# One of a quad's 32 exponential tiles moved from ScalarE to GpSimd as a power of two, with a reordered quad and GpSimd in written order

## The chip, the core and the metric

The kernel runs on one core of a Trainium2 chip. The metric is the device time of one execution in microseconds (us), here the median of the runs shown. TensorE (PE) multiplies matrices into PSUM, ScalarE (ACT) applies functions such as the exponential, VectorE (DVE) and GpSimd (POOL) do elementwise work, SyncE (SP) issues the transfers, which 16 DMA engines carry. PEld is the loading of weights into PE.

## What is computed

Four residual layers over a sequence of 2048 rows of 512 numbers, with 32 heads of 16. Layers 0 and 2 attend within a window of 256 keys, layers 1 and 3 over all 2048 keys.

```python
def _B_ref(x, wqkv, wo):                      # _A_ref: the same with a causal window of 256
    qkv = (x @ wqkv).reshape(B, S, 3, H, Dh) ...
    scores = jnp.einsum("bhqd,bhkd->bhqk", q, k) * Dh ** -0.5
    p = softmax(scores)
    o = jnp.einsum("bhqk,bhkd->bhqd", p, v)
    return o.transpose(...).reshape(B, S, D) @ wo
x = x + _A_ref(_layernorm(x), A_wqkv, A_wo)
x = x + _B_ref(_layernorm(x), B_wqkv, B_wo)
x = x + _A_ref(_layernorm(x), A_wqkv, A_wo)
x = x + _B_ref(_layernorm(x), B_wqkv, B_wo)
```

## The kernel before

**A quad.** The full layers (1 and 3) work by chunks `c` of 512 queries and, in a chunk, by quads `qd` of four heads: 4 x 8 quads in a layer. A quad goes through 16 key tiles `j` of 128 keys. For each `j` there are two pairs of heads `pr`, and for each pair one score tile `s` of 128 x 1024 (128 keys, two heads by 512 queries), so a quad has 32 score tiles. `exps` (L714) makes a score tile: PE writes it by eight matmuls into one of two PSUM buffers (`ps_s`), and ACT reads it and writes the exponential `e` to SBUF (L735), into one of six buffers (`EB`). A score tile can be written when ACT has read the one two before it. The queries and keys have been extended beforehand by rows that hold a bound, so that the scores come out already shifted and no row maximum is taken.

**The product with the values.** `attn_full` (L767) runs the 16 steps. Its product with the values of step `j` (the `pv` of a step, L779: eight matmuls in the program, 16 in the records, into the two accumulators `acc`) comes later than its exponentials. `attention` keeps products in a line `pvq`, and `flush(1)` lets all but the youngest go whenever a step has written its first score tile (the `yield None` after pair 0). So in the steady state PE's order is: score tile (j,0), product j-2, score tile (j,1), side work, score tile (j+1,0). After the last product of a quad, `epilogue` (L683) has DVE add the two accumulators (`sa`, L415 and L416), transpose, and divide by the sum; the next quad's first product overwrites the accumulators and so waits for `sa`.

**Side work.** Beside the quads, `Side` hands PE small pieces of the projections of this and of the next layers (`project`, `values`, `wo`, `wo_part`), eight or sixteen matmuls at a time between two score tiles. In the full layers they all go through one PSUM tile of two banks, `PH["halves"]` (the side bank, named `b` in the trace). When one of its results is complete, DVE reads both banks (`join`, or L677 and L653), and only then can PE write the next one. What is left of a chunk's side work at the chunk's end (in layer 1: at the layer's end) is done there by `sd.finish()`, one piece after the other, with no score tile between.

**Order.** In the full layers PE and DVE run in the order in which the program issues them. The planner keeps a clock (`clock[0]`, 1.8 us a step) and its estimates of when DVE is free (`vt_`) and results are ready, and places the pieces by them. The orders of ACT, POOL and SP are made by a scheduler, and each engine and queue takes its instructions strictly in its order.

**Loads.** `load_full` (L744) loads a quad's queries `qt` (256 KB, two buffers) and its keys as two halves `kt` of 512 KB (key tiles 0 to 7 and 8 to 15) in a ring of three buffers. The second half for a quad goes into the buffer that the first half of the quad before it held, so it can be loaded only when that quad has written its last score tile from key tiles 0 to 7. All these loads are issued by SP.

**POOL** in the full layers has only the squares of queries and keys (`sq`, L521), whose sums PE takes by `hsum` (L543), and the low halves of the outputs (`oh`, L712).

Of the kernel before, what the change touches and what calls it, by code (L numbers as in the profile page):

```python
# [9 lines left out]
F32 = mybir.dt.float32  # L10
# [23 lines left out]
EB, XB, XNB, WB, VB, OB = 6, 4, 4, 2, 3, 5  # L34
RINGS = WB, VB
L_MIN = 2.0 ** -90
# [153 lines left out]
def fast_path(ctx, tc, flag, a_x, a_wqkv, a_wo, b_wqkv, b_wo, out):  # L190
# [13 lines left out]
    ctx.push(ps_x)  # L204
    dp = pool("scr", 1, space=bass.MemoryType.DRAM)
# [5 lines left out]
    XC, XN, V, O, OT, KM, PH = {}, {}, {}, {}, {}, {}, {"free": 0.0, "busy": False}  # L211
    WT, ST, pend = {}, {}, []
    VQ, vt_ = [deque() for _ in range(4)], [0.0]
# [15 lines left out]
    def soon(chain, us, f):  # L229

        if PH["full"]:
            VQ[chain].append((clock[0], us, f))
        else:
            f()

    def drain(upto=None):

        if upto is not None:
            for q in VQ[:upto]:
                while q:  # L240
                    vec(q[0][1])
                    q.popleft()[2]()
            return
        while vt_[0] <= clock[0] + 0.2:
            q = next((q for q in VQ if q), None)
            if q is None:
                return
            vec(q[0][1])
            q.popleft()[2]()
# [21 lines left out]
    zeros = cp.tile([P, QC], F16, name="zeros")  # L271
# [15 lines left out]
    nc.gpsimd.memset(zeros, 0.0)  # L287
# [15 lines left out]
    def fill(t, key, c0=0, c1=1):  # L303
        r4 = lambda d0, d1: rows(t).rearrange("h (d b) (c n) -> h d b c n", b=4, n=QC)[:, d0:d1, 3]
        for c in range(c0, c1):
            if key:
                nc.sync.dma_start(r4(0, 1)[:, 0, c], ones[:H])
                nc.sync.dma_start(r4(1, DH)[:, :, c], zeros[:H, None, :].broadcast_to([H, DH - 1, QC]))
            else:
                nc.sync.dma_start(r4(1, DH)[:, :, c], ones[:H, None, :].broadcast_to([H, DH - 1, QC]))  # L310
# [31 lines left out]
    def verify(ty, s):  # L342

        am = vp.tile([P, D], F32, name=f"wa{ty}_{s}", tag="wa", bufs=1)
        for k in range(NC):
# [4 lines left out]
            yield from turns(3, (1.1, lambda: nc.vector.tensor_reduce(am[:, f], raw.rearrange("p k f -> p f k"), axis=AX.X, op=ALU.max,  # L350
                                                                      apply_absolute_value=True)))

        def bounds():
            at = vp.tile([P, D], F32, name=f"wt{ty}_{s}", tag="wc", bufs=1)
            nc.vector.transpose(at, am)
            mx = vp.tile([P, D // 32], F32, name=f"wx{ty}_{s}", tag="wx")
            nc.vector.tensor_reduce(mx, at.rearrange("p (b r) -> p b r", r=32), axis=AX.X, op=ALU.max)
            nc.vector.tensor_tensor(wlow, wlow, mx, ALU.min)
            nc.vector.tensor_tensor(whigh, whigh, mx, ALU.max)
        yield from turns(3, (1.8, bounds))  # L360
# [12 lines left out]
    def phase(l):  # L373

        PH["full"], PH["win"] = l is not None and l % 2 == 1, l is not None and l % 2 == 0
# [53 lines left out]
    def norm(l, c, xs, tail=False):  # L429

        mv, y, nb, out = ST[l, c][1], [], [], []

        def scales():
            y.append(rsqrt(nc, vp, f"{l}_{c}", mv[:, :, 1]))
# [4 lines left out]
        def parts(i):  # L439
            xn = vp.tile([P, D], F32, name=f"xn{l}_{c}_{i}", tag="xn", bufs=1)  # L440
# [37 lines left out]
    def project(l, s, c, act, ht=None):  # L478
# [5 lines left out]
        xc = XC[l, c]  # L484
        if s == 0:
# [6 lines left out]
        for t in range(NHT) if ht is None else (ht,):  # L492
# [19 lines left out]
            def parts(t=t, sp=None if full else sp, j=j if full else None):  # L512
                if full:
                    sp = vp.tile([P, 2, QC], F16, name=f"sp{n}_{t}", tag="sp", bufs=3)
                    nc.vector.tensor_copy(sp[:, 0], j)  # L515
                    nc.vector.tensor_tensor(sp[:, 1], j, sp[:, 0], ALU.subtract)
                sq = vp.tile([P, QC], BF16, name=f"sq{n}_{t}", tag="sq", bufs=NHT)
# [77 lines left out]
    def key_shift(l, ht=None):  # L595
# [6 lines left out]
        nc.vector.tensor_scalar(m[r], ones[r], kx[r], -0.515, op0=ALU.mult, op1=ALU.mult)  # L602
# [39 lines left out]
    def wo(l, c, tail):  # L642
# [4 lines left out]
        for i in range(4):  # L647
# [11 lines left out]
            yield -MM if PH["full"] else -12 * MM  # L659
        if PH["full"]:  # L660
            yield from norm(l + 1, c, xs, tail)

    def wo_part(c, t):
# [6 lines left out]
        for i in range(4):  # L670
# [7 lines left out]
            nc.sync.dma_start(out[0, k * P:(k + 1) * P, :] if t == NHT - 1 else xd[k], xs[i])  # L678
            yield -MM

    def epilogue(l, c, qd, a):
# [25 lines left out]
        def parts():  # L707
            o = vp.tile([P, QC], F32, name=f"o{n}", tag="o", bufs=1)
            nc.vector.transpose(o, OT.pop(t).rearrange("p b u d -> p (b u d)"))
            hl = O[l, c, t] = wp.tile([P, 2, QC], F16, name=f"oh{n}", tag="ohl", bufs=OB)  # L710
# [4 lines left out]
        if u:  # L715
            soon(1, 1.2, parts)

    def exps(name, kt, qt, pr, pieces):
# [15 lines left out]
        e = pp.tile([P, 2, QC], F32, name=f"e{name}", tag="e", bufs=EB)  # L734
        nc.scalar.activation(e[:, :, w0:w1], ps[:, :, w0:w1], AF.Exp, scale=SCALE)  # L735
        return e

# [29 lines left out]
    def attn_full(l, c, qd, kt, qt, a):  # L767
        for j in range(NT):
            es_ = []
            for pr in range(2):  # L770
# [4 lines left out]
            def pv(j=j, es_=es_):  # L775
                for h in range(4):
                    for r in range(2):
                        k = slice(R * r, R * r + R)
                        nc.tensor.matmul(acc[r][32 * h:32 * h + DH + 1, :], V[l, qd // 4, j // 8][k, j % 8, 4 * (qd % 4) + h, :],  # L779
                                         es_[h // 2][k, h % 2, :], start=(j == 0), stop=(j == NT - 1),  # L780
# [39 lines left out]
    class Work:  # L820
# [7 lines left out]
        def ready_at(self):  # L828
# [12 lines left out]

            if self.norm and not self.begun and NB:
# [40 lines left out]
    class Side:  # L883
# [65 lines left out]
        def share(self):  # L949

            self.budget = min(self.budget + max((self.cost - self.spent) / max(self.steps - 3 - self.k, 1), self.least), 0.75)
            self.lag = max(self.lag - 0.42, -0.3)
            if pend and not PH["busy"] and clock[0] >= max(PH["free"], pend[0][0]):
# [32 lines left out]
    def attention(l, works):  # L986
# [5 lines left out]
        for t in range(NHT if l == 3 else 1):  # L992
            for c in range(NQ):
                qds = range(2 * t, 2 * t + 2) if l == 3 else range(NQD)
                if l == 1:

                    sd = sd or Side(NT * NQD // 2, works[0], works[1], 0.33)
                    while ("Q", 1, c) not in DONE:
# [4 lines left out]
                ops = load(l, c, qds[0])  # L1003
                for qd in qds:
# [4 lines left out]
                    a = acc[qd % 2 if win else 0]  # L1009
                    began, u = clock[0], 0  # L1010
                    for f in (attn_win if win else attn_full)(l, c, qd, *ops, a):
# [6 lines left out]
                        clock[0] = max(clock[0], began + (2.4 if win else 1.8))  # L1018
# [16 lines left out]
                if not win:  # L1035
# [155 lines left out]
    for l in range(4):  # L1191
# [5 lines left out]
        else:  # L1197
            with tc.manual_schedule(engines={mybir.EngineType.PE, mybir.EngineType.DVE}):
# [42 lines left out]
```

## Time and profile before

| what | value |
|---|---|
| runs | 2759.74 and 2760.26 us, median 2760.0 us |
| the profiled execution | 2759.5 us, span 2757.7 us |
| granted TensorE clock, mean | 0.988 |
| busy share of the span | PE 91%, ACT 86%, DVE 40%, PEld 40%, POOL 19% |

The page gives the busy time of each engine, the span in 40 slices of 69 us with a digit for the busy tenths of each engine, the chain of work that ended last, and the groups of instructions with their mean durations and the idle time ahead of them. In the timeline a row is: start, duration, engine, line, operation, output and inputs, how many, and in brackets the idle time ahead and what ended it. Matmuls overlap in the array, so PE's speed is read from the distance between starts, not from the duration of one. ACT's records overlap as well: the distance of two starts is what a tile costs.

### The profile page before, as it was taken

To read this page: it belongs to the slowest core of one execution; us is meant where nothing else is said; L and a number is where in the kernel's file an instruction comes from. 1 tells how busy PE (TensorE), PEld (TensorE's weight loads), DVE (VectorE), ACT (ScalarE), POOL (GpSimd) and SP (SyncE) were. 2 spreads that over 40 slices of the span, in tenths; PEclk is the share of its full clock that TensorE was granted. 3 is DMA by queue.
4 is the path that set the end of the run, shared out by engine and by line. 5 is a ranking of instruction groups with operands and counts; after the bars stand their busy time and mean duration, and the time that the engine had idled before them with its cause. 6 is when DMAs were issued, how large, how long until landed. Compare 5 with 4: busy or idle time off the path is not lost.

```text
span 2757.7 us, 112292 instructions
## 1 busy us (share of the span) xinstructions
PE 2496.1 (91%) x50513; PEld 1100.3 (40%) x50513; DVE 1094.9 (40%) x2314; ACT 2362.9 (86%) x2683; POOL 515.8 (19%) x1074
## 2 busy tenths in 40 slices
PE   7888989999989999999998898899899999998987
PEld 3233334444433344444443333534444444433332
DVE  5564554122343335325326566323333333333333
ACT  4556654899999999999995667399999999999997
POOL 1445552001000000100105678100000000000000
PEclk9999999999999999999999999999999999999999
DMA  8888856322342224324225565623232333333332
GB/s 286 226 241 240 244 178 191 96 83 82 100 120 79 86 93 137 102 78 126 93 73 169 157 181 143 175 72 109 84 107 90 98 97 104 112 104 123 114 120 103
DMA packets 335035, 359.67 MB, mean 130 GB/s; under 512 B 113616, under 2 KB 250320, under 8 KB 328144
## 3 DMA queue, kind: packets, MB, share of 16 engines
q1 hardware_dynamic: 334544, 352.40, 42.3%
q8 instruction: 397, 6.50, 1.0%
q14 instruction: 94, 0.77, 0.1%
HBM read 239.60 MB, written 96.99 MB: 122 GB/s over the span
## 4 chain that ended last, share of the span: by engine, by line
ACT 56%; PE 23%; issue 11%; DVE 5%; DMA 3%; POOL 2%; SPq 0%; ACTq 0%; DVEq 0%; POOLq 0%
ACT e L735 55%; PE b L402 10%; PE acc L812 3%; PE acc L779 3%; PE bs L402 2%; PE s L731 2%; PE s L727 2%; PE b L399 1%; POOL e L802 1%; POOL e L805 1%; DMA qt<-qs 1%; DMA kt<-kw 0%; DMA wr<-in_A_wo_dram 0%; DVE ot L694 0%; DMA w<-wd 0%
## 5 line engine op out<-in xcount | busy, mean ns | idle before, releaser
L735 ACT ACTIVATE e<-s 128x1024 f32<-128x1024 f32 (+2 forms) x2432 | 2238.8, 1058 | 121.0 <-PE s L731 95.3
L779 PE MATMUL acc<-e,vt 64*17 64x512 f32 x16384 | 1085.0, 590 | 1.3 <-issue 1.3
L727 PE MATMUL s<-qt,kt 64*32 64x512 f16 x16384 | 849.0, 380 | 130.4 <-ACT e L735 106.6
L727 PEld LDWEIGHTS <-kt 64*32 64x32 f16 x16384 | 406.7, 89 | 944.2 <-issue 868.8
L779 PEld LDWEIGHTS acc<-e,vt 64*17 64x17 f32 x16384 | 280.5, 92 | 61.1 <-issue 1.5
L805 POOL TENSOR_SCALAR_AFFINE_SELECT e<-e 128x256 f32<-128x256 f32 x512 | 224.9, 446 | 196.5 <-ACT e L735 195.4
L802 POOL TENSOR_SCALAR_AFFINE_SELECT e<-e 128x256 f32<-128x256 f32 x448 | 198.1, 449 | 114.1 <-ACT e L735 112.3
L712 POOL TENSOR_TENSOR oh<-o,oh 128x512 f16<-128x512 f32 x31 | 36.1, 1165 | 938.1 <-DVE oh L711 884.8
L812 PE MATMUL acc<-e,vt 128*17 128x384 f32 (+2 forms) x2816 | 204.7, 396 | 5.3 <-POOL e L802 4.0
L731 PE MATMUL s<-qt,kt 64*128 64x384 f16 (+2 forms) x1408 | 129.0, 280 | 64.0 <-ACT e L735 38.2
L415 DVE TENSOR_SCALAR sa<-acc 128x512 f32<-128x512 f32 x64 | 44.3, 692 | 335.4 <-PE acc L779 335.4
L402 PE MATMUL b<-xc,w 128*128 128x512 f16 x696 | 166.1, 390 | 7.0 <-DMA w<-wd 5.8
L677 DVE SCALAR_TENSOR_TENSOR x<-b,x 128x512 f32<-128x512 f32 x122 | 83.9, 688 | 193.0 <-PE b L399 189.8
L402 PEld LDWEIGHTS <-w 128*128 128x128 f16 x816 | 77.4, 100 | 122.8 <-issue 35.8
L521 POOL TENSOR_TENSOR sq<-sp 128x512 bf16<-128x512 f16 x28 | 41.0, 1463 | 442.2 <-DVE sp L515 427.6
L506 ACT ACTIVATE sp<-b 128x512 f16<-128x512 f32 x58 | 34.7, 598 | 103.3 <-PE b L402 91.2
L731 PEld LDWEIGHTS <-kt 64*128 64x128 f16 x1408 | 54.4, 94 | 167.6 <-issue 137.0
L521 POOL TENSOR_TENSOR sq_h<-sp_h 128x512 bf16<-128x512 f16 x27 | 40.1, 1484 | 409.8 <-DVE sp_h L515 409.8
L399 PE MATMUL b<-wo,oh 64*32 64x512 f16 x2592 | 109.9, 376 | 6.2 <-DVE x L677 3.1
L399 PE MATMUL b<-xc,w 64*32 64x512 f16 x2688 | 110.9, 376 | 3.0 <-DVE j L416 2.3
L399 PE MATMUL b<-xc,w_h 64*32 64x512 f16 x2592 | 104.4, 376 | 4.1 <-DVE km L562 3.9
L415 DVE TENSOR_SCALAR j_h<-b 128x512 f32<-128x512 f32 x27 | 18.7, 691 | 218.7 <-PE b L399 187.6
(136 smaller groups left out, 1874.8 us busy)
## 6 DMA issues: line engine op xcount, KB each, us to landing
kt<-kf SPq DMA_DIRECT2D x128, 512.0 KB
qt<-qs SPq DMA_DIRECT2D x128, 256.0 KB
xd<-x SPq DMA_DIRECT2D x96, 256.0 KB
x<-xd SPq DMA_DIRECT2D x96, 256.0 KB
w<-wd SPq DMA_DIRECT2D x22, 1024.0 KB
kt<-kw SPq DMA_DIRECT2D x64, 256.0 KB
qs<-sp SPq DMA_DIRECT2D x48, 256.0 KB
wo<-wd SPq DMA_DIRECT2D x12, 1024.0 KB
```

Of the source, the lines that this page charges most:

```text
L399: nc.tensor.matmul(ps[g:g + 32, r], a[k, g:g + 32], b[k], start=(i == 0), stop=(i == len(pairs) - 1), skip_group_check=True)
L402: nc.tensor.matmul(ps, a, b, start=(i == 0), stop=(i == len(pairs) - 1))
L415: nc.vector.tensor_scalar(dst, ps[0], scale, None, op0=ALU.mult)
L521: nc.gpsimd.tensor_tensor(sq, sp[:, 0], sp[:, 0], ALU.mult)
L677: nc.vector.scalar_tensor_tensor(xs[i], p, 1 / WS, xs[i], op0=ALU.mult, op1=ALU.add)
L727: nc.tensor.matmul(ps[g:g + 32, h], kt[R * h:R * h + R, pr, kc + g:kc + g + 32], qt[R * h:R * h + R, pr], start=True, stop=True, skip_grou ...
L731: nc.tensor.matmul(ps[:, h, s0:s0 + wd_], kt[R * h:R * h + R, pr, kc:kc + P], qt[R * h:R * h + R, pr, qc:qc + wd_], start=True, stop=True)
L735: nc.scalar.activation(e[:, :, w0:w1], ps[:, :, w0:w1], AF.Exp, scale=SCALE)
L779: nc.tensor.matmul(acc[r][32 * h:32 * h + DH + 1, :], V[l, qd // 4, j // 8][k, j % 8, 4 * (qd % 4) + h, :], es_[h // 2][k, h % 2, :], star ...
L802: nc.gpsimd.affine_select(v, v, pattern=[[0, 2], [-1, P]], compare_op=ALU.is_gt, fill=0.0, base=0, channel_multiplier=1)
L805: nc.gpsimd.affine_select(v, v, pattern=[[0, 2], [1, P]], compare_op=ALU.is_ge, fill=0.0, base=0, channel_multiplier=-1)
L812: nc.tensor.matmul(a[32 * h:32 * h + DH + 1, q * P:(q + nb) * P], V[l, (4 * c + j) // 4][:, j % 4, 4 * qd + h, :], es_[h // 2][:, h % 2, s ...
```

## The change

In the full layers, key tile `DJ` = 7 is taken out of its place and done last in the quad (`js`). Of its two score tiles, the one of pair 0 no longer goes to ACT. `unit` has PE write it, at some earlier step, into the side bank; DVE scales it by SCALE times log2(e), clamps it at -126 and writes it to SBUF (a new tile `d`, two buffers); POOL raises two to it, in place, in two instructions of 128 x 512. The product of key tile 7 then reads `d` for pair 0 and ACT's `e` for pair 1. `units` decides at which step: for the next quad from 6 us (by the planner's clock) into the present one, as soon as the side bank is free, and for the first quad of a chunk at once. The planner's own cost for POOL's two instructions is `XP` = 9.0. The last step of a quad has one ACT tile, no `yield None`, and is planned as 0.9 us.

POOL joins PE and DVE in running in written order. The `e` tiles get a pool of their own, with six buffers in the window layers and five in the full ones. To make room, `zeros` becomes a part of `ones` and the weight check (`verify`) works in tiles of 128 columns: 32 times five DVE instructions instead of 32 plus 8 times four. `key_shift` takes one small DVE instruction more. The planner gets a few conditions: an output tile is not overwritten before it has been used (`OFREE`), sums of squares wait for POOL's planned time (`PH["sq"]`), and side work is held while a unit waits for the side bank. All 64 quads of the two layers have a unit in the changed program: ACT has 64 instructions fewer, DVE 64 and POOL 128 more for it.

```diff
-EB, XB, XNB, WB, VB, OB = 6, 4, 4, 2, 3, 5
+EB, XB, XNB, WB, VB, OB = (6, 5), 4, 4, 2, 3, 5
+DJ = NT // 2 - 1
+UNITS = 1
+XP = 9.0
...
+    def unit(u):
+        pr = len(u["e"])
+        ps = PH["halves"]
+        for g in range(0, P, 32):
+            for h in range(2):
+                nc.tensor.matmul(ps[g:g + 32, h], u["kt"][R * h:R * h + R, pr, DJ % 8 * P + g:DJ % 8 * P + g + 32],
+                                 u["qt"][R * h:R * h + R, pr], start=True, stop=True, skip_group_check=True)
+        spent(0.27)
+        vec(1.4)
+        PH["free"] = max(clock[0] + 0.6, vt_[0])
+        t = PH["ep"].tile([P, 2, QC], F32, name=f"d{n}", tag="d", bufs=2)
+        nc.vector.tensor_scalar(t, ps, SCALE * LOG2E, -126.0, op0=ALU.mult, op1=ALU.max)
+        pt_[0] = max(pt_[0], vt_[0]) + XP
+        for h in range(2):
+            nc.gpsimd.tensor_tensor(t[:, h], two.broadcast_to([P, QC]), t[:, h], ALU.pow)
+        u["e"].append(t)
...
     def attn_full(l, c, qd, kt, qt, a):
-        for j in range(NT):
+        js = [j for j in range(NT) if j != DJ] + [DJ]
+        for j in js:
             es_ = []
-            for pr in range(2):
+            if j == DJ:
+                es_ = list(UX.popleft()["e"])
+            PH["step"] = 1.8 - 0.9 * len(es_)
+            for pr in range(len(es_), 2):
                 es_.append(exps(f"{l}_{c}_{qd}_{j}_{pr}", kt[j // 8], qt, pr, [(j % 8 * P, 0, QC, 0)]))
                 if pr == 0:
                     yield None
...
-                                         es_[h // 2][k, h % 2, :], start=(j == 0), stop=(j == NT - 1),
+                                         es_[h // 2][k, h % 2, :], start=(j == js[0]), stop=(j == js[-1]),
...
+                if not win:
+                    expect(l, c, qds[0], *ops, 0.0)
...
+                    if nxt and not win:
+                        expect(l, c, qd + 1, *nxt, 6.0)
...
-            with tc.manual_schedule(engines={mybir.EngineType.PE, mybir.EngineType.DVE}):
+            with tc.manual_schedule(engines={mybir.EngineType.PE, mybir.EngineType.DVE, mybir.EngineType.Pool}):
```

**Where it moves instructions: the end of a quad.** This is PE's order from quad 2 to quad 3 of chunk 1 in layer 1, one row for each run of like rows. A name `s_1_2_15_1` is chunk, quad, key tile and pair (the last number is the buffer's); a row that reads `s` stands for the eight matmuls of a score tile, a row on `acc` for the four matmuls with one of a step's two exponential tiles. Before:

```order
L727 MATMUL s_1_2_15_1_13728<-qt_1_2_12382,kt_1_2_1_12386 32x512
...
L727 MATMUL s_1_3_0_0_13745<-qt_1_3_13088,kt_1_3_0_13090 32x512
...
L779 MATMUL acc_81<-e_1_2_14_0_13678,vt_0_1_5232 17x512
...
L779 MATMUL acc_81<-e_1_2_14_1_13702,vt_0_1_5232 17x512
...
L727 MATMUL s_1_3_0_1_13769<-qt_1_3_13088,kt_1_3_0_13090 32x512
...
L779 MATMUL acc_81<-e_1_2_15_0_13713,vt_0_1_5232 17x512
...
L779 MATMUL acc_81<-e_1_2_15_1_13737,vt_0_1_5232 17x512
...
L727 MATMUL s_1_3_1_0_13793<-qt_1_3_13088,kt_1_3_0_13090 32x512
```

And at the same place in the changed program:

```order
L755 MATMUL s_1_2_7_1_13668<-qt_1_2_12304,kt_1_2_0_12306 32x512
...
L755 MATMUL s_1_3_0_0_13701<-qt_1_3_13012,kt_1_3_0_13014 32x512
...
L847 MATMUL acc_81<-e_1_2_14_0_13599,vt_0_1_5230 17x512
...
L847 MATMUL acc_81<-e_1_2_14_1_13618,vt_0_1_5230 17x512
...
L847 MATMUL acc_81<-e_1_2_15_0_13631,vt_0_1_5230 17x512
...
L847 MATMUL acc_81<-e_1_2_15_1_13650,vt_0_1_5230 17x512
...
L755 MATMUL s_1_3_0_1_13728<-qt_1_3_13012,kt_1_3_0_13014 32x512
...
L847 MATMUL acc_81<-d_1_2_0_12758,vt_0_0_4501 17x512
...
L847 MATMUL acc_81<-e_1_2_7_1_13677,vt_0_0_4501 17x512
...
L755 MATMUL s_1_3_1_0_13752<-qt_1_3_13012,kt_1_3_0_13014 32x512
```

The quad now ends with a single score tile, after which no product is let go. The two products that wait then (14 and 15) both stand between the next quad's first and second score tile, where one stood before. The same holds at all 62 places where a quad follows a quad in its layer. The last score tile of the quad also reads `kt_1_2_0`, the first half of the keys, which before had its last reader at key tile 7 in the middle of the quad.

**The end of layer 1**, on PE. Before, the last score tile is followed by the last two products:

```order
L727 MATMUL s_3_7_15_1_28645<-qt_3_7_27293,kt_3_7_1_27297 32x512
...
L779 MATMUL acc_81<-e_3_7_14_0_28605,vt_1_1_5653 17x512
...
L779 MATMUL acc_81<-e_3_7_14_1_28624,vt_1_1_5653 17x512
...
L779 MATMUL acc_81<-e_3_7_15_0_28635,vt_1_1_5653 17x512
...
L779 MATMUL acc_81<-e_3_7_15_1_28654,vt_1_1_5653 17x512
```

In the changed program 304 matmuls of side work (the values of layer 2's chunk 2, in the side bank, 96 for each filling) and the sums of squares `sq` stand there first:

```order
L755 MATMUL s_3_7_7_1_28525<-qt_3_7_27124,kt_3_7_0_27126 32x512
...
L417 MATMUL b_5730<-wv_2_0_0_26774,xc_2_25732 32x512
...
L566 MATMUL b_5730<-sq_1_2_0_27285,hsum 32x512
...
L847 MATMUL acc_81<-e_3_7_14_0_28442,vt_1_1_5658 17x512
...
L847 MATMUL acc_81<-e_3_7_14_1_28461,vt_1_1_5658 17x512
```

Such a run of side work without score tiles also stands at the ends of two chunks of layer 3, where there was none before: 160 matmuls of 256 columns (values) after quad 3 of chunk 1, and 96 of 512 columns (`wo`, 24 for each filling) with 192 of 256 columns (values) after quad 3 of chunk 3.

**SP's order** in layer 3, chunk 0, around the loads for its quad 5. Before, the second half of quad 4's keys, three rows on other data, then quad 5's queries and the first half of its keys:

```order
L752 DMA kt_0_4_1_44441<-kf 128x2x1024
L588 DMA qs_0_101<-m_0_2_44109 8x512
...
L748 DMA qt_0_5_44443<-qs_0_101 128x2x512
L752 DMA kt_0_5_0_44445<-kf 128x2x1024
...
L752 DMA kt_0_5_1_44447<-kf 128x2x1024
```

In the changed program:

```order
L816 DMA kt_0_4_1_44707<-kf 128x2x1024
L812 DMA qt_0_5_44709<-qs_0_101 128x2x512
L816 DMA kt_0_5_0_44711<-kf 128x2x1024
L703 DMA xd<-x_12_44320 128x512
L482 DMA x_0_44795<-xd 128x512
...
L816 DMA kt_0_5_1_44713<-kf 128x2x1024
```

The first of these rows now waits for the last score tile of the quad before, and the two behind it wait with it; `unit` of quad 5 reads their data six score tiles later. In layer 3 seven such units stand six tiles after the release, in layer 1 five stand eight tiles after it, the others ten or more.

105 lines of the change are left out of this document (74 added, 31 removed).

## The prediction

> **What bounds the kernel now.** I read the page first (busy shares and slices), then ACT's exponentials by stage, then the chain of waits and the timeline of one quad's end.
>
> ```profile
> span 2757.7 us, 112292 instructions
> PE 2496.1 (91%) x50513; PEld 1100.3 (40%) x50513; DVE 1094.9 (40%) x2314; ACT 2362.9 (86%) x2683; POOL 515.8 (19%) x1074
> ACT  4556654899999999999995667399999999999997
> POOL 1445552001000000100105678100000000000000
> L735 ACT ACTIVATE e<-s 128x1024 f32<-128x1024 f32 (+2 forms) x2432 | 2238.8, 1058 | 121.0 <-PE s L731 95.3
> ```
>
> The two stretches of 9s in ACT's row are the full layers, which hold two thirds of the span. There POOL is nearly idle. The stages of ACT's line, columns: span, ACT busy and count, granted clock, DMA share, GB/s:
>
> ```profile
> 1100.00:1300.00 200.00, 198.22 (x216) 1.00 0.34 102
> 2100.00:2300.00 200.00, 197.28 (x215) 1.00 0.31 93
> ```
>
> In both layers ACT is busy 99% of the time with exponentials alone: it is the bound, and 216 tiles in 200 us leave next to nothing between them. The busy share of PE over the whole span says less, since its matmuls overlap. What one tile costs, and how close PE follows, is read in the chain of waits (start, duration, what) and the timeline, at a place where one quad follows another in layer 1:
>
> ```profile
> 701.16 0.87 ACT e L735
> ...
> 702.08 0.71 ACT e L735
> ...
> 703.00 0.87 ACT e L735
> ...
> 703.91 1.03 ACT e L735
> 704.94 0.04 issue
> 704.98 0.60 ACT e L735
> ```
>
> ```profile
> 702.30 0.41 PE L727 MATMUL s<-qt,kt 64*32 64x512 f16 x8 [0.35 <-ACT e L735]
> 702.51 1.05 PE L779 MATMUL acc<-e,vt 64*17 64x512 f32 x16
> 703.37 0.41 PE L727 MATMUL s<-qt,kt 64*32 64x512 f16 x8
> 703.59 1.05 PE L779 MATMUL acc<-e,vt 64*17 64x512 f32 x16
> 704.44 0.41 PE L727 MATMUL s<-qt,kt 64*32 64x512 f16 x8
> 704.66 0.63 PE L399 MATMUL b<-xc,w 64*32 64x512 f16 x16
> 704.74 0.69 DVE L415 TENSOR_SCALAR sa<-acc 128x512 f32<-128x512 f32 x1 [1.88 <-PE acc L779]
> 705.09 0.41 PE L727 MATMUL s<-qt,kt 64*32 64x512 f16 x8
> ```
>
> Five prices follow, from starts. A tile costs ACT (703.91 - 702.08) / 2 = 0.915 us. A score tile costs PE 0.21 (702.30 to 702.51), a product with the values 0.86 (702.51 to 703.37), sixteen side matmuls 0.43 (704.66 to 705.09). ACT starts at the earliest 0.54 after PE starts the tile (704.44 to 704.98), and PE may refill a buffer 1.14 after ACT started on it (701.16 to 702.30). So a buffer's circle takes 1.14 + 0.54 = 1.68 of the 1.83 that two tiles give: PE may be 0.15 late, no more. The third tile here was late: 704.98 where 703.91 + 0.915 = 704.82 was due. A quad's end costs 0.16 before the change.
>
> **The sum.** It is made against the profiled execution, 2759.5 us (span 2757.7), which lies 0.5 under the median of 2760.0.
>
> *ACT loses 64 tiles:* 64 x 0.915 = **-58.6 us**. That is the ceiling, 2.1%.
>
> *The quad's end.* I count from ACT's start on the last tile before key tile 7's (0.00), with the prices above. The single tile of key tile 7 follows at 0.92. PE can write the next quad's first tile at 1.14; ACT takes it at 1.83, in time. Behind it now stand two products: 1.14 + 0.21 + 2 x 0.86 = 3.07 for the second tile, so ACT starts it at 3.61, where 2.75 was due. The product of key tile 7 follows (3.07 + 0.21 + 0.86 = 4.14), the third tile reaches ACT at 4.68 instead of 3.61 + 0.915 = 4.53. Together 1.02 late, against 0.16 before: 0.86 at each of 62 places, **+53.3**. The reason is the missing pause after a single tile; a slack of 0.15 cannot hide a product of 0.86. So the end of the quad gives back nearly the whole tile.
>
> *The unit's own work.* PE writes the same eight matmuls as before, in a slot that side work would have had: 0 while that slot exists. In the first quad of 15 chunks of layer 3 it stands between the next quad's second tile and the last product, where there is no slot: 0.21, and DVE reads the side bank ahead of `sa`, so the accumulators come free about 0.25 later. 15 x 0.46 = **+7**. DVE's reading of 1024 numbers from PSUM costs what `km` of the same size does:
>
> ```profile
> L562 DVE TENSOR_REDUCE km<-b 128x1 f32<-128x1024 f32 x3 | 3.7, 1225 | 5.0 <-PE b L543 5.0
> L712 POOL TENSOR_TENSOR oh<-o,oh 128x512 f16<-128x512 f32 x31 | 36.1, 1165 | 938.1 <-DVE oh L711 884.8
> L521 POOL TENSOR_TENSOR sq<-sp 128x512 bf16<-128x512 f16 x28 | 41.0, 1463 | 442.2 <-DVE sp L515 427.6
> L677 DVE SCALAR_TENSOR_TENSOR x<-b,x 128x512 f32<-128x512 f32 x122 | 83.9, 688 | 193.0 <-PE b L399 189.8
> ```
>
> 64 x 1.23 on an engine that is 40% busy is hidden, apart from the places named. No row shows a power. POOL's nearest instructions of the size take 1.17 and 1.46, so a unit takes at least 2.3 us; the planner charges 9.0. I take 9.0, since a power is more work than a product. It is hidden either way: a quad lasts 32 x 0.915 = 29 us, and its product of key tile 7 stands at least 17 score tiles (15 us) after that in nearly all quads, so up to some 24 us it would cost nothing. `sq` and `oh` queue behind it on POOL; their readers on PE stand 3 or more score tiles after they would be done at 9.0, save three `sq` behind which PE waits today as well, 1.2 us in all:
>
> ```profile
> L543 PE MATMUL b<-sq_h,hsum 64*32 64x512 bf16 x54 | 10.3, 377 | 2.1 <-POOL sq_h L521 1.2 <-DVE x L677 0.8 <-DVE vt L416 0.2
> ```
>
> That makes 0 for POOL.
>
> *Left-over side work.* The orders show three runs without score tiles that were not there. Each filling of the side bank ends in two DVE instructions (0.69 each by L677's row) and some 0.25 of signals, 1.65 in all, before PE may write again. End of layer 1: 304 matmuls, 304 / 16 x 0.43 = 8.2, four turns 6.6, one product more 0.9: 15.7. Layer 3, 160 matmuls of half the columns: 2.2 and one turn of half size 1.1, less the 0.7 that PE waits there anyway: 2.6. Layer 3, 96 and 192: 2.6 + four turns 6.6 + 2.6 + 1.1 - 0.7 = 12.2. Sum **+30.5**, since ACT has nothing to do meanwhile. At the very end of layer 3 one more turn, a product and eight matmuls: **+3**.
>
> *The loads.* At a quad's end SP now issues three loads at once, 512, 256 and 512 KB, 1.31 MB. What the queue moves in such a burst (core's row: span, then busy times, clock, DMA share, GB/s):
>
> ```profile
> 705.00:709.00 4.00, 3.88 (x120) 1.82 (x111) 2.88 (x8) 4.00 (x5) 0.00 (x0) 1.00 0.81 252
> 760.80:767.20 6.40, 4.70 (x112) 1.91 (x111) 4.39 (x10) 6.40 (x8) 0.00 (x0) 1.00 0.51 166
> ```
>
> The second row holds an issue of 1 MB from its first to its last byte, 166 GB/s x 6.4 us. At that rate 1.31 MB takes 7.9 us; at the 252 GB/s of the first row, inside a burst, 5.2. From the release at 0.7 on the count above the data is there at 5.9 to 8.6. A unit six tiles on is due at 7.5 (six tiles of 0.915 and the lost 1.02 after 1.14), one eight tiles on at 9.4. So seven units wait 0 to 1.1, and PE and with it ACT wait too; should a second transfer of 256 KB lie between, 1.6 more. I take 1.1 for six of the seven (one stands behind left-over work), **+7**; between 0 and 17. The five buffers of `e` delay the next quad's first tile by 0.2, within the 0.86 already lost. The weight check's additional instructions lie on DVE beside a layer of 950 us: 0.
>
> Sum: -58.6 + 53.3 + 7 + 30.5 + 3 + 7 = +42, **2802 us**, 1.5% slower.
>
> **The port rule.** POOL is busy in the window layer in the middle of the span (5 to 8 tenths in its row of slices), with short instructions, and the same DVE instruction, two inputs from SBUF, takes longer there. DVE's row in 1100 to 1300 us, then in 1500 to 1700, then POOL's instruction:
>
> ```profile
> L699 DVE TENSOR_TENSOR lsum<-lsum,ot 128x16 f32<-128x16 f32 x6 | 1.1, 179 | 0.0
> ```
>
> ```profile
> L699 DVE TENSOR_TENSOR lsum<-lsum,ot 128x16 f32<-128x16 f32 x22 | 7.2, 326 | 0.0
> ```
>
> ```profile
> L805 POOL TENSOR_SCALAR_AFFINE_SELECT e<-e 128x256 f32<-128x256 f32 x512 | 224.9, 446 | 196.5 <-ACT e L735 195.4
> ```
>
> It is 0.15 us longer beside POOL instructions of 0.45: what a wait for the rest of one would give. The Trainium skill has the rule for it (SBUF — State Buffer, Who interferes with whom): the port pair that the two engines share is held for a whole instruction, and a VectorE instruction with two SBUF inputs waits until a GpSimd instruction that reads SBUF is done. The trace agrees in direction; how long a power would hold it no run here shows.
>
> **Rivals.**
> 1. *POOL holds DVE up.* In the first quad of a chunk in layer 3, `lmin`, `lsum` and `op` stand on DVE between the two units' readings. If they wait for both halves of the first power (till 14 us on the count above at 9.0), the second unit's reading ends at about 16, and PE, which needs the side bank at some 13, waits 3: seven to 15 places, +20 to +45, 2822 to 2847; I write 2830. For it: the row of `lsum`. Against it: the power may be shorter, and POOL may let DVE in between.
> 2. *Not slower: the second product is hidden.* If PE got both products done before the tile was due, the 53.3 would go and the sum would be 2749; at 0.18 per place instead of 0.86 it breaks even. It needs score buffers that are free earlier; the row at 702.30, where PE waits 0.35 for ACT, speaks against it.
> 3. *The loads and left-overs cost less:* the loads land at 252 GB/s, and half of the left-over work overlaps: -22, 2780.
> 4. *The power takes over 24 us:* key tile 7's product waits in the first quads and the squares with it; at 30 us some 6 us in 16 quads, 2900.
>
> **How the numbers follow.** Chances: the forecast 0.47, rival 1 0.27, rival 2 0.08, rival 3 0.14, rival 4 0.04. The forecast's own range is 2788 to 2820 (0.1 on 0.86 at 62 places, and the loads from 0 to 17). The range of 2770 to 2842 takes in rival 3 and most of rival 1. Two per cent, about what a measurement of this kernel can tell from no change, ends at 2704.8 and 2815.2. Faster by that much would need the whole ceiling: 0.02. Slower: 0.18 of the forecast's 0.47, 0.23 of rival 1, rival 4: 0.45. Within: 0.53.
>
> **What would show it.** Right: at a quad's end ACT's starts show 1.8 us once where 0.92 is usual; the chain has PE's share up and ACT's down; 64 exponentials fewer; a gap in ACT of some 15 us at the end of layer 1. Wrong: starts at a quad's end that keep 0.92; PE rows of unit or product that wait for POOL; `lmin` rows on DVE of several us, which is rival 1.

## The result, and the profile after

The changed kernel takes 11950.2 us (11947.05 and 11953.27), 4.33 times the time before, with an interval of 4.311 to 4.348. The forecast was 2802.

The page of the changed kernel: busy time of the engines, three rows of slices (one slice is now 299 us), the chain that ended last, and six groups of instructions (busy, mean ns of one, then the idle time ahead of them and what ended it).

```profile
PE 2704.2 (23%) x50513; PEld 1134.0 (9%) x50513; DVE 1189.3 (10%) x2479; ACT 2329.1 (19%) x2619; POOL 10980.0 (92%) x1203
ACT  5411111211111112112341111211012111021110
POOL 4599999999999999999878999898998889988889
PEclk9865555655666556656785555656556555565555
POOL 79%; issue 10%; PE 6%; ACT 3%; DVE 1%; DMA 1%; SPq 0%; ACTq 0%; DVEq 0%; POOLq 0%
L782 POOL TENSOR_TENSOR d<-two,d 128x512 f32<-128x512 f32 x128 | 10482.9, 81917 | 439.4 <-DVE d L779 439.4
L763 ACT ACTIVATE e<-s 128x1024 f32<-128x1024 f32 (+2 forms) x2368 | 2205.7, 1049 | 9205.3 <-PE s L755 8762.3
L847 PE MATMUL acc<-d,vt 64*17 64x512 f32 x512 | 174.5, 866 | 5128.9 <-POOL d L782 5128.9
L566 PE MATMUL b<-sq_h,hsum 64*32 64x512 bf16 x54 | 13.7, 498 | 2842.5 <-POOL sq_h L544 2840.8
L566 PE MATMUL b<-sq,hsum 64*32 64x512 bf16 x56 | 11.6, 505 | 864.5 <-POOL sq L544 861.5
L417 PE MATMUL b<-wo,oh 64*32 64x512 f16 x2592 | 126.0, 394 | 154.3 <-POOL oh L740 145.9
```

The bound has changed its engine. POOL's row reads 8 and 9 through both full layers, where it read 0 and 1, and ACT's reads mostly 1 and 2, where it read 9. The row of L782 says why: one power of 128 x 512 takes 81.9 us, a unit 163.8, where 9.0 had been taken. The 128 powers are 10483 of the 11945 us. The last four rows show how POOL's time reaches the others. PE waits 5129 us for the product of key tile 7. It waits 2841 and 862 us for squares (`sq_h` and `sq`), instructions of 1.1 to 1.2 us that stand behind powers in POOL's order, and 146 us for the low halves of the outputs. Together that is 8977 us. ACT's 9205 us of idle time are nearly all (8762) ended by PE's next score tile: PE stands, so nothing comes.

Two answers of the trace on the rival in which POOL holds DVE up. First POOL's row in the timeline (start, duration), then DVE's rows inside it:

```profile
663.02 163.81 POOL L782 TENSOR_TENSOR d<-two,d 128x512 f32<-128x512 f32 x2
```

```profile
667.85 0.18 DVE L725 TENSOR_TENSOR lmin<-lmin,ot 128x16 f32<-128x16 f32 x1
667.95 0.17 DVE L726 TENSOR_TENSOR lsum<-lsum,ot 128x16 f32<-128x16 f32 x1
668.53 0.43 DVE L732 TENSOR_TENSOR op<-ot,r 128x256 f32<-128x256 f32 x1
```

DVE instructions with two inputs from SBUF run at their usual length 5 us into a power that lasts another 77. Of each of these three lines, 46 instructions in the whole trace lie inside a power; the longest took 0.19, 0.19 and 0.43 us. DVE was not held.

### The profile page after: what moved, and what is told of

It is laid out like the page before. It is cut to its first block, busy times and chain, and to the rows that moved or that the text cites. A ratio compares the mean times of both kernels' runs of the same rounds, so it can differ in the third digit from the quotient of the medians.

```text
span 11945.3 us, 112446 instructions
## 1 busy us (share of the span) xinstructions
PE 2704.2 (23%) x50513; PEld 1134.0 (9%) x50513; DVE 1189.3 (10%) x2479; ACT 2329.1 (19%) x2619; POOL 10980.0 (92%) x1203
## 4 chain that ended last, share of the span: by engine, by line
POOL 79%; issue 10%; PE 6%; ACT 3%; DVE 1%; DMA 1%; SPq 0%; ACTq 0%; DVEq 0%; POOLq 0%
POOL d L782 79%; ACT e L763 3%; PE b L420 2%; PE acc L847 1%; PE acc L880 1%; PE s L755 0%; PE bs L420 0%; PE s L759 0%; POOL oh L740 0%; PE b L417 0%; DVE d L779 0%; POOL sq L544 0%; POOL sq_h L544 0%; POOL e L873 0%; POOL e L870 0%
## 5 line engine op out<-in xcount | busy, mean ns | idle before, releaser
L782 POOL TENSOR_TENSOR d<-two,d 128x512 f32<-128x512 f32 x128 | 10482.9, 81917 | 439.4 <-DVE d L779 439.4
L763 ACT ACTIVATE e<-s 128x1024 f32<-128x1024 f32 (+2 forms) x2368 | 2205.7, 1049 | 9205.3 <-PE s L755 8762.3
L847 PE MATMUL acc<-d,vt 64*17 64x512 f32 x512 | 174.5, 866 | 5128.9 <-POOL d L782 5128.9
L847 PE MATMUL acc<-e,vt 64*17 64x512 f32 x15872 | 1169.7, 619 | 0.7 <-issue 0.7
L755 PE MATMUL s<-qt,kt 64*32 64x512 f16 x15872 | 924.2, 400 | 123.5 <-ACT e L763 104.4
L566 PE MATMUL b<-sq_h,hsum 64*32 64x512 bf16 x54 | 13.7, 498 | 2842.5 <-POOL sq_h L544 2840.8
L585 DVE TENSOR_REDUCE km<-b 32x1 f32<-32x1024 f32 (+3 forms) x26 | 25.8, 991 | 1352.7 <-PE b L566 1206.9
```

What stands on the lines that cost most here:

```text
L755: nc.tensor.matmul(ps[g:g + 32, h], kt[R * h:R * h + R, pr, kc + g:kc + g + 32], qt[R * h:R * h + R, pr], start=True, stop=True, skip_grou ...
L782: nc.gpsimd.tensor_tensor(t[:, h], two.broadcast_to([P, QC]), t[:, h], ALU.pow)
```

## The experiments

**1. Only the power's duration taken away.** A multiplication of the same inputs in its place; all orders stay.

```diff
-        nc.vector.tensor_scalar(t, ps, SCALE * LOG2E, -126.0, op0=ALU.mult, op1=ALU.max)
+        nc.vector.tensor_scalar(t, ps, SCALE * LOG2E, 0.5, op0=ALU.mult, op1=ALU.max)
...
-            nc.gpsimd.tensor_tensor(t[:, h], two.broadcast_to([P, QC]), t[:, h], ALU.pow)
+            nc.gpsimd.tensor_tensor(t[:, h], two.broadcast_to([P, QC]), t[:, h], ALU.mult)
```

> The changed kernel with POOL's power replaced by a multiplication of the same two inputs and size, and DVE's clamp at 0.5 in place of -126 so that the numbers stay positive; it leaves the power out, all else and every order stays. Theory A, the power's own duration (81.92 us for one of 128 x 512, 164 for a unit) is all that went wrong, and the other terms of the sum hold: 2802 us, ACT's starts at a quad's end show 1.8 us once, some 15.7 us without tiles at the end of layer 1. Rival B, the second product at a quad's end is hidden: 2749. Rival C, something besides the power's duration holds the changed kernel up (the written order of POOL, the waits of the squares): several thousand us still, or well above 2850.

Measured: 2806.6 us, 1.0156 of the time before (1.0139 to 1.0173). Theory A holds to 5 us: 9144 us of the changed kernel's time are the power's duration, and what is left is the forecast's own sum (its terms follow further down). POOL's and ACT's rows with the multiplication, and the chain of waits over one quad's end:

```profile
L782 POOL TENSOR_TENSOR d<-two,d 128x512 f32<-128x512 f32 x128 | 132.3, 1054 | 760.0 <-DVE d L779 727.7 <-DVE v L49 31.1 <-DVE kx L604 1.2
L763 ACT ACTIVATE e<-s 128x1024 f32<-128x1024 f32 (+2 forms) x2368 | 2196.9, 1052 | 201.7 <-PE s L759 116.5 <-PE acc L847 52.0 <-PE s L755 20.2
```

```profile
1030.80 1.10 ACT e L763
...
1031.94 0.41 PE s L755 x8
1032.35 0.89 PE acc L847 x12
...
1033.32 1.02 ACT e L763
...
1034.41 1.03 ACT e L763
...
1035.48 0.60 ACT e L763
```

The forecast counted from ACT's start on the tile ahead of key tile 7's, here 1030.80 (the single tile of key tile 7 runs beside PE's rows and is not on the chain). The next quad's second tile was to start 3.61 later, the third 4.68. They start at 1034.41 and 1035.48: 3.61 and 4.68. The first tile was put at 1.83 and starts at 2.52: its buffer is the fifth one back, which the product of key tile 14 still reads, and ACT's row names that product for 52 us of its idle time. Since the second tile is late by PE's order anyway, this costs nothing further.

**2. One product behind the single tile.** A pause after it as well, so that the bunched products are spread.

```diff
-            for pr in range(len(es_), 2):
+            for pr in range(first, 2):
...
-                if pr == 0:
+                if pr == first:
                     yield None
```

> As the one with the multiplication (the power is left out), and the quad's last step pauses after its single tile as well, so that by PE's order one product, not two, stands between the first and the second score tile of the next quad at 62 places. Theory A, a second product of 0.86 us costs its full length at each place: 53 us less than without the pause, about 2749. Rival B, the second product was hidden, or its wait comes back at the next tile: no more than 10 us less.

Measured: 2818.3 us, 1.0203 (1.0186 to 1.0220), so 12 us slower than without the pause. Theory A falls, and B does not say why it is slower. The profiled execution is the fastest of the four, 2812.1 us, and so only 6 us slower than the one profiled without the pause. By ACT's starts it spends 6.5 us less in layer 1 (939.1 for 945.6), 3.7 less in layer 3 (975.7 for 979.4) and 6.6 less ahead of and between them, but 22.9 more after layer 3's last score tile (48.6 for 25.7). Two things work against each other. The loss at a quad's end shrinks only in part, from 1.02 us to a median of 0.75 in layer 1: three products (14, 15 and 7) still stand between four tiles, since the program lets the last one go at the end of the next quad's first step. And the planner, asked to go on at other points, leaves 224 matmuls of side work for the very end instead of 56. DVE's timeline there, first, second and last pair, with PE's work as the wait between them:

```profile
2762.33 1.42 DVE L702 SCALAR_TENSOR_TENSOR x<-b,x 128x512 f32<-128x512 f32 x2 [3.87 <-PE b L417]
2764.71 1.42 DVE L702 SCALAR_TENSOR_TENSOR x<-b,x 128x512 f32<-128x512 f32 x2 [0.96 <-PE b L417]
...
2788.59 1.42 DVE L702 SCALAR_TENSOR_TENSOR x<-b,x 128x512 f32<-128x512 f32 x2 [1.60 <-PE b L417]
```

Ten turns of 2.4 to 3.0 us through the one side bank, with no exponential beside them.

**3. No unit in any quad.** The rest of the change stays.

```diff
-UNITS = 1
+UNITS = 0
```

> The changed kernel with no unit in any quad: all 32 tiles on ACT, nothing left out; key tile 7 last, POOL in written order, five buffers of exponentials, the weight check in small tiles and the planner's conditions stay. Theory A, these cost nothing: 2755 to 2768. Rival, the written order on POOL or the late second half of the keys costs by itself: 2775 or more, with PE rows that wait for POOL or for a load.

Measured: 2764.7 us, 1.0009 (0.9999 to 1.0018): no difference that this can tell. POOL's written order, five buffers, key tile 7 at the end and the smaller tiles of the weight check cost together 5 us at most, by the upper end of the interval.

**4. One of the two instructions a power.**

```diff
-            nc.gpsimd.tensor_tensor(t[:, h], two.broadcast_to([P, QC]), t[:, h], ALU.pow)
+            nc.gpsimd.tensor_tensor(t[:, h], two.broadcast_to([P, QC]), t[:, h], ALU.pow if h == 0 else ALU.mult)
```

> The changed kernel with the first of a unit's two POOL instructions a power and the second a multiplication (it leaves half of the powers out). Theory A, POOL's own time bounds the full layers, and the power costs the same whoever waits: 64 x (81.9 + 1.2) = 5320 us on POOL, and with the window layers and the weight check (some 900 to 1500 us that POOL's units do not cover) 6200 to 6800. Rival, the loss is a wait for each unit of a fixed kind (signals, order) and not its busy time: above 9000.

Measured: 6769.6 us (one execution). Theory A holds. Taking 64 powers away saved (11950.2 - 6769.6) / 64 = 80.9 us each. A power less the multiplication in its place is 81.92 - 1.05 = 80.9 as well, so these 64 stood wholly in series. The other 64 give (6769.6 - 2806.6) / 64 = 61.9 us each, so of these some 19 us each lay beside other work.

**5. The power by itself.** A small kernel of its own, of which these are the lines that matter (`g` is POOL, `b` the broadcast two):

```python
o = new("q512"); g.tensor_tensor(o, b(512), x, ALU.pow)
o3 = new("q32p"); g.tensor_tensor(o3[:32], b(512, 32), x[:32], ALU.pow)
o4 = new("qzero"); g.tensor_tensor(o4, b(512), zero, ALU.pow)
o6 = new("qmul"); g.tensor_tensor(o6, b(512), x, ALU.mult)
```

> POOL's power by itself, on data that nothing else waits for: 128 x 512, 128 x 256, 128 x 64, 32 partitions x 512, the exponent zero everywhere, a bf16 result, and the multiplication of the same inputs on POOL and on DVE. It computes none of the reference. Theory A, the price goes by the number of columns whatever the data (0.160 us a column): 82 us, 41, 10.2; the zero exponent and the bf16 result 82 as well; the multiplication on POOL about 1.05. For 32 of the 128 partitions it is 82 if the price goes by columns alone, 20 if it goes by numbers. Rival, the price depends on the data or on the read of a broadcast column: the zero exponent well under 82, or the multiplication well over 1.05.

POOL's groups, one instruction each, with duration in us and in ns:

```profile
L33 POOL TENSOR_TENSOR qbf<-two,x 128x512 bf16<-128x512 f32 x1 | 82.1, 82124 | 0.0
L31 POOL TENSOR_TENSOR qzero<-two,zero 128x512 f32<-128x512 f32 x1 | 81.9, 81920 | 1.1 <-DVE zero L22 1.1
L27 POOL TENSOR_TENSOR q<-two,x 128x512 f32<-128x512 f32 x1 | 81.9, 81920 | 0.0
L30 POOL TENSOR_TENSOR q32p<-two,x 32x512 f32<-32x512 f32 x1 | 81.9, 81906 | 0.0
L28 POOL TENSOR_TENSOR q<-two,x 128x256 f32<-128x256 f32 x1 | 41.1, 41115 | 0.0
L29 POOL TENSOR_TENSOR q<-two,x 128x64 f32<-128x64 f32 x1 | 10.5, 10515 | 0.0
L32 POOL TENSOR_TENSOR qmul<-two,x 128x512 f32<-128x512 f32 x1 | 1.0, 1029 | 0.0
```

Theory A holds, by columns alone: 0.160 us a column, whether the exponent is zero or not, for 32 partitions as for 128. The broadcast base is not the reason, since the multiplication reads it too and takes 1.03.

**6. The same function without a power**, to some 4%. Scaled and rounded to a whole number, whose bits are read as a number.

```diff
-            nc.gpsimd.tensor_tensor(t[:, h], two.broadcast_to([P, QC]), t[:, h], ALU.pow)
+            nc.gpsimd.tensor_scalar(t[:, h].bitcast(I32), t[:, h], 2.0 ** 23, 126.9425 * 2.0 ** 23, op0=ALU.mult, op1=ALU.add)
```

> The changed kernel with the power made otherwise: POOL takes y x 2^23 + 126.9425 x 2^23, rounded to a whole number, and these bits are read as a number, which is 2^y to within some 4% (straight lines between powers of two). Nothing else is changed, and the output is the reference's to that. Theory A, the power's duration alone made the time: as with the multiplication, 2806 within 6 us, if POOL's instruction takes between 1 and 10 us. Rival, an instruction that writes whole numbers is as slow on POOL as the power: several thousand us.

POOL's group:

```profile
L782 POOL TENSOR_SCALAR d<-d 128x512 int32<-128x512 f32 x128 | 81.2, 634 | 782.1 <-DVE d L779 744.4
```

Measured: 2807.7 us, 1.0180 (1.0165 to 1.0196), as with the multiplication; 0.63 us an instruction. The exponential's tile can be made off ACT, to some 4%, at no cost that POOL's duration causes, and the kernel is slower than before all the same: the 58.6 us that ACT saves are given back at the quads' ends and in left-over work.

**7. The missing tile in the middle of the quad.** With the bits, here and in the next one. The planner's figures follow the new order, in lines that are not shown: its cost for POOL's two instructions is 3.0, a unit has to be done by key tile 7, and side work is spread over 15 steps of a quad.

```diff
-        js = [j for j in range(NT) if j != DJ] + [DJ]
+        js = list(range(NT))
...
-            for pr in range(len(es_), 2):
+            for pr in range(first, 2):
...
-                if pr == 0:
+                if pr == first:
                     yield None
...
-                        elif u:
+                        elif u and PH["step"] > 1:
                             sd.step()
```

> As the one that makes the bits, with key tile 7 in its natural place in the middle of the quad, a pause behind its single tile, and no side work in that step. 61 of 64 quads have a unit by the order. Theory A, the loss at a quad's end was two products bunched between two tiles, and a place with one product behind each tile loses 0.16 for each: 2764 (the kernel with no unit) - 61 x 0.915 + 61 x 0.16 = 2718, and then what the order shows as left-over side work: 17 at the end of layer 1, 15 and 6 in layer 3, 28 at its end, 2784 in all. Rival, the second product's length is lost wherever the tile is missing (0.86 each): 43 more, 2827.

Measured: 2789.5 us, 1.0110 (1.0094 to 1.0125); 2784 was expected by theory A, 2827 by the rival. The chain of waits at one place where a tile is missing shows ACT alone:

```profile
595.53 0.71 ACT e L763
...
596.45 0.87 ACT e L763
...
597.36 1.03 ACT e L763
...
598.44 0.56 ACT e L763
...
599.36 0.71 ACT e L763
```

The start at 598.44 follows 1.08 after the one before, 0.16 more than 0.915, and that is all that the place costs. Layer 1 as a whole bears it out: with 29 units it is 25.7 us shorter than in the kernel with no unit (921.2 for 946.9), 0.89 for each tile of 0.915. Most of the rest is side work without slots: against the kernel with no unit, 14.3 us more between the end of layer 1's tiles and the first of layer 3, 26.4 more behind the last tile of layer 3, 37.6 more of late starts within layer 3. Of these 37.6, some 29 lie at two runs of side work there (at 2121 and from 2468 us); the other 9 are not split here.

**8. Units only where a slot is left for the side work.** As the one before, with units in 18 quads of layer 1.

```diff
+        if not (l == 1 and (c < 2 or c == 2 and qd < 4)):
+            UX.append(dict(n=f"{l}_{c}_{qd}", quad=(l, c, qd), kt=kts[DJ // 8], qt=qt, e=[], shut=True, ready=clock[0] + us))
+            return
```

> As the one with key tile 7 in the middle, with units in only 18 quads of layer 1 (chunks 0 and 1 and half of chunk 2), so that no side work is left over by the order. Theory A, the place costs 0.16 of the 0.915 and the left-over work was the rest: 2764 - 18 x 0.755 = 2750, 0.4% faster than before, and faster than the kernel with no unit by 0.5%. Rival, the missing tile's time is given back at once wherever it is: 2760 to 2765.

ACT's group of exponentials:

```profile
L763 ACT ACTIVATE e<-s 128x1024 f32<-128x1024 f32 (+2 forms) x2414 | 2225.2, 1054 | 121.3 <-PE s L759 100.6 <-PE s L755 16.1 <-POOL e L873 1.4
```

Measured: 2747.3 us, 0.9954 (0.9941 to 0.9968): faster than both kernels. ACT does 18 tiles fewer and idles 121.3 us, as before the change (121.0), so little is given back. 18 x (0.915 - 0.16) is 13.6 us, and the median lies 13.7 under that of before. The agreement to the tenth is luck: the kernel with no unit is the nearer one to compare with, and the median lies 17.4 under its 2764.7. By ACT's starts layer 1 is 15.1 us shorter than in that kernel (931.8 for 946.9), 0.84 for each of the 18 tiles, and no work is left over at the ends of the full layers: the stretch from layer 1's last tile to layer 3's first takes 337.5 us for 339.1, and the one behind layer 3's last 21.4 for 21.3.

**9. How long may a unit take?** The power on 64, then on 96 of each instruction's 512 columns, multiplication on the rest.

```diff
-            nc.gpsimd.tensor_tensor(t[:, h], two.broadcast_to([P, QC]), t[:, h], ALU.pow)
+            nc.gpsimd.tensor_tensor(t[:, h, :64], two.broadcast_to([P, 64]), t[:, h, :64], ALU.pow)
+            nc.gpsimd.tensor_tensor(t[:, h, 64:], two.broadcast_to([P, QC - 64]), t[:, h, 64:], ALU.mult)
```

> The changed kernel with the power on 64 of each instruction's 512 columns and a multiplication on the other 448, so it leaves seven eighths of the powers out. By the power measured alone (10.5 us for 64 columns) and a multiplication of 1.03 for 512, a unit takes POOL 2 x (10.5 + 0.9) = 22.8 us. Theory A, as the prediction had it, a unit of under some 24 us costs the product of key tile 7 nothing, and what queues behind it on POOL neither: 2806 as with the multiplication, within 6. Rival, the squares and sums that queue behind a unit of 23 us hold PE up: 2820 or more, with PE rows that wait for POOL's squares.

> As the one before with 96 columns of power for each instruction (it leaves the other powers out): a unit takes 2 x (15.6 + 0.85) = 32.9 us, more than the 28.4 that a quad of 31 tiles gives. Theory A, POOL's own time is now the bound of the full layers: 32 x 32.9 + 40 of squares and low halves = 1093 us a layer against some 962 with the multiplication, 2806 + 2 x 131 = 3070. Rival, the units' lead of one quad is spent only in the first quads of a chunk, as the prediction had it (some 9 us at 16 places): 2950.

Measured: 3118.1 us with 64 columns, 1.1298 (1.1276 to 1.1319), and 3595.8 with 96 (one execution). Theory A falls in both. The rival holds for 64 columns, with 312 us above the multiplication's 2806.6 where at least 14 had been named; for 96 columns neither sum came near. PE's rows on POOL's results, 64 columns and then 96 (there with the other squares, `sq`):

```profile
L566 PE MATMUL b<-sq_h,hsum 64*32 64x512 bf16 x54 | 13.5, 490 | 271.8 <-POOL sq_h L544 270.1 <-DVE vt L434 1.7
L848 PE MATMUL acc<-d,vt 64*17 64x512 f32 x512 | 71.8, 598 | 3.4 <-POOL d L783 3.4
```

```profile
L566 PE MATMUL b<-sq_h,hsum 64*32 64x512 bf16 x54 | 13.7, 498 | 490.8 <-POOL sq_h L544 489.1 <-DVE vt L434 1.7
L566 PE MATMUL b<-sq,hsum 64*32 64x512 bf16 x56 | 7.3, 426 | 86.1 <-POOL sq L544 83.1 <-DVE vt L434 3.1
L848 PE MATMUL acc<-d,vt 64*17 64x512 f32 x512 | 114.5, 648 | 121.7 <-POOL d L783 121.7
```

At 23 us a unit, the product that reads it waits 3.4 us in the whole program. The squares behind it in POOL's order keep PE waiting 270. At 33 us the wait for squares grows to 489 and 83, and now the product waits 122. Of the 789 us above the multiplication these rows hold 694; the rest is not split here.

**10. The squares taken out from behind the units.** As the one with 64 columns, the squares of the full layers on DVE; PE's order is the same.

```diff
-                    nc.gpsimd.tensor_tensor(sq, sp[:, 0], sp[:, 0], ALU.mult)
+                    (nc.vector if PH["full"] else nc.gpsimd).tensor_tensor(sq, sp[:, 0], sp[:, 0], ALU.mult)
```

> The kernel with 64 columns of power (seven eighths of the powers left out) and the squares of the full layers on DVE, not behind the units on POOL; PE's order is the same. Theory A, the 312 us between that kernel and the multiplication were PE waiting for squares that queue behind a unit of 23 us on POOL, and the product of key tile 7 itself is in time: 2806 to 2850. Rival, the product or the low halves of the outputs wait as well and the time is lost there instead: 2950 or more.

PE's row on the squares:

```profile
L566 PE MATMUL b<-sq_h,hsum 64*32 64x512 bf16 x54 | 10.4, 377 | 2.7 <-DVE vt L434 2.2 <-DVE sq_h L544 0.6
```

Measured: 2822.5 us, 1.0234 (1.0217 to 1.0251). Theory A holds: 296 of the 312 us go when the squares no longer stand behind the units. What the other 16 are is not shown.

## Why the prediction was wrong, and where it was right

**The step that failed** is the one on POOL's power: "I take 9.0, since a power is more work than a product. It is hidden either way." The term of the sum was 0, and it measured 9144 us (changed kernel less the one with the multiplication). Two things in it were wrong.

- *The price.* 2.3 us was a lower bound from the nearest rows; 9.0 was the planner's figure, a number that the program assumes and no measurement. No row bounded the power from above, and none could: POOL's rows of that size were all of another kind of work. The multiplication beside it takes 1.03 us, the power 81.9 (experiment 5), 80 times as much. The range took no end from this term at all.
- *The threshold.* "Up to some 24 us it would cost nothing" was the deadline of the unit's own reader. Experiments 9 and 10 agree with that deadline: at 23 us the product waits 3.4 and 3.5 us in all, at 33 us 122, and nothing between was run. But POOL works in order, and the squares behind the unit are due much earlier. The prediction had that in hand, "3 or more score tiles after they would be done at 9.0", which is some 12 us, and did not use it as the limit. So rival 4, the right mechanism, got 24 us for its threshold, 2900 for its time and 0.04 for its chance. At 33 us it gives 3596, and at 164 it gives 11950.

**The other terms**, by the kernel with the multiplication and that of before, from ACT's starts in the two profiled executions:

| term | forecast | measured | by |
|---|---|---|---|
| 64 tiles fewer | -58.6 | -58.6 | 64 x 0.915 |
| quads' ends | +53.3 | +53.3 | 62 x 0.86: the next quad's three tiles together 1.02 late (median in each layer), 0.16 before |
| left over, layer 1's end | +15.7 | +14.9 | last tile of layer 1 to first of layer 3: 352.6, before 337.7 |
| left over in layer 3 | +14.8 | +19.5 | two places, 14.9 and 4.6 |
| very end | +3 | +4.7 | behind the last tile: 25.7, before 21.0 |
| units in first quads, loads | +14 | +7.1 | all other late starts, not told apart |
| ahead of layer 1's first tile | 0 | +5.2 | 500.7, before 495.5 |
| sum | +42 | +46 | 2804.0 - 2757.7 |

The quad's end was counted from five prices of one place and came out to the hundredth at the usual place. The sum came out to 5 us partly by luck, since the loads were taken too high and the left-over work in layer 3 too low. That its first tile would be late by 0.2 for want of a buffer was a miss (0.69), hidden as the prediction said, by the second tile's delay. The loads hardly cost anything: with the multiplication PE waits 1.6 us for keys ahead of its units, where 7 had been taken, and 0.8 ahead of its score tiles, as before. (By the prediction's own terms a unit six tiles on was due at 1.14 + 6 x 0.915 + 1.02 = 7.65, not 7.5; that would have made the term smaller by 1.) What lies ahead of layer 1 moves by some microseconds from kernel to kernel (498.7 with no unit, 494.7 with the bits) and is no term of the change.

**The rivals.** Rival 1 (POOL holds DVE up) is wrong: the rows of `lmin` and `lsum` inside a power read 0.18 and 0.17 us, and none of the 46 of each line reads more than 0.19. The Trainium skill's rule behind it (SBUF — State Buffer, Who interferes with whom: a VectorE instruction with two SBUF inputs contends with a GpSimd instruction that reads SBUF, and the shared port pair is an exclusive lock) does not describe this instruction; the measurement decides. Rival 2 (the second product is hidden) is wrong by experiment 1. The reason that the prediction gave for the 0.86, the missing pause, was only part of it: the pause alone left 0.75 of the 1.02 (experiment 2), and a place where every tile is followed by one product or one piece of side work costs 0.16 (experiment 7). Rival 3 was right about the loads and wrong about the left-over work. Rival 4 decided the case, at a price that it did not have.

**What was to show it wrong** did: the rows of the product that waits for POOL.

## What to carry to other kernels

An operation that no row shows has no upper bound, and a planner's constant is none; run that one instruction by itself first, or let the forecast say from which duration on it decides and keep that end in the range. On an engine that works in order, a long instruction is limited by the earliest deadline of anything queued behind it, not by that of its own reader. Here a tile taken off the pacing engine paid only where the engine that feeds it kept one piece of work between two tiles, and where the side work still found its slots: 64 such tiles cost 47 us, 18 well placed ones, with the approximate power, gained 14.

## What the runs showed of the hardware

POOL's power (a base of two from a broadcast column, exponents in f32) takes 0.160 us a column (one f32 number in each partition): 10.5 us for 64 columns, 41.1 for 256, 81.9 for 512, the same for 32 partitions as for 128, for an exponent of zero, and 82.1 for 512 with a bf16 result. POOL's scaling with two constants and rounding to whole numbers takes 0.63 us for the size at which its multiplication of two tensors takes 1.03 to 1.05. DVE instructions with two inputs from SBUF ran beside the power at their usual length, 0.17 to 0.19 us for 128 x 16 and 0.43 for 128 x 256. POOL's instructions ran in their order: squares of 1.2 us behind a unit of 23 us kept PE waiting 270 us in all. The granted TensorE clock was lower in the runs in which PE idled more: 0.987 with PE busy 90% of the span (multiplication), 0.939 at 82% (64 columns), 0.887 at 73% (96), 0.705 at 39% (one power in two), 0.615 at 23% (the changed kernel). PE holds only 6% of the changed kernel's chain, so little of the time can hang on that.
